# Strassen output product on one core: the loads of k, v and q queued behind the turns of q

## The chip, the core and the metric

The kernel runs on one core of one Trainium2 chip. The metric is device time in microseconds (us), the lower the better. A core has a matrix engine (TensorE, PE in the profile, with its weight loads as PEld), a vector engine (VectorE, DVE), an activation engine (ScalarE, ACT), a general engine (GpSimd, POOL) and an engine that here only issues transfers (SyncE, SP). Each works through its own instructions in order and waits on semaphores for the others. Transfers (DMAs), plain ones and those that transpose, are issued from the queues of these engines and are carried out by 16 DMA engines.

## The reference

```python
# q, k, v: (8, 8, 576, 64) float32; w_in: (512, 2048); w_out: (2048, 512)
k_p = k.reshape(B, H, 72, 8, D).mean(axis=3)
v_p = v.reshape(B, H, 72, 8, D).mean(axis=3)
scores = scale * np.matmul(q, k_p.transpose(0, 1, 3, 2))
scores = scores - np.max(scores, axis=-1, keepdims=True)
attn = np.exp(scores)
attn = attn / (np.sum(attn, axis=-1, keepdims=True) + 1e-09)
x = np.matmul(attn, v_p)          # then (B*S, H*D) = (4608, 512)
h = x @ w_in
out = (h - np.tanh(h)) @ w_out    # (4608, 512) float32
```

## The kernel before

The work has two parts that run beside each other: attention, batch by batch (8 batches of 576 rows, 8 heads), and a two-layer product, group by group (9 groups of 512 tokens). The attention output, turned so that features lie on partitions, is the tile xT, a ring of three groups. The first group and the first two batches are handled ahead of the loop; the rest is the loop `for g in range(1, NG)` (L926). A pass of this loop is called pass g below. In pass g the matrix engine computes group g, and the attention of batch nb = g + 1 is computed between its products; the raw inputs of batch nn = g + 2 are loaded. So passes 1 to 5 load, passes 1 to 6 do attention, and passes 7 and 8 only do their groups.

A pass on PE begins with the up projection: seven `h_pair` and two `h_one`, 64 matmuls (L529) of w1b by xT into PSUM. ACT takes the tanh (L541), DVE subtracts it and leaves Gt (L542). Then comes the output product, in 14 steps of u, eight matmuls each (L585): seven products of sums of blocks (Strassen's scheme) in place of eight. In steps 0 to 4, after the eight matmuls, `scores(nb, u)` runs: two halves of 288 columns of a score tile (L348), whose right-hand side is qT, then the exponentials on ACT (L367). In steps 6, 7, 8, 9 and 11 `av` computes 128 rows of the attention output each, and a DMA transpose from SP's queue (L433) turns it into xT. In step 6 POOL sums k and v of batch nn over the pools of 8 (`pool_k`, L247 to L255, then `pool_v`, L266 to L290). Stores of the group's output (L602) follow at the end of the pass.

A group has 512 tokens and a batch 576, so the up projection of pass g + 1 reads 448 - 64 g rows of batch g + 1 at the most: of the five turns of x that pass g issues, the first three are needed in pass 1 to 2, two in passes 3 and 4, one after that.

The order of all instructions is that of the program text (`manual_schedule`), engine by engine. What concerns the change is the queue of SP. In pass g it issues, in this order:

- at p = 0, `k_dma_transpose(nb)` (L331): one DMA that turns the summed k, kd, into kT, which POOL then places into KB for the scores (L299 to L303)
- at p = 0, if there is a batch nn, `load_k(nn)` (L137 of 1024 KB, L146 of 128 KB) and `load_v(nn)` (L137 of 1024 KB, L141 four times of 32 KB)
- at p = 2 (in pass 1 at p = 3, c being p - 1 there), `q_dma_transpose(nb)` (L203): five DMA transposes of q_bf into qT, one for each block of 128 or 64 rows of q
- there too, if there is a batch nn, `load_q(nn)` (L170 of 1024 KB, L162 of 128 KB)
- in the product steps the five turns of x (L433), then the stores (L602)

q_bf is the bf16 copy of q that ACT casts in three parts (`q_cast_part`, L192 and L197) ahead of `h_pair` for p = 0, 1, 2. The buffer of raw q, q_raw, is a single one; k_raw, v_raw, KB and qT have two buffers each.

Of the kernel before, what the change touches and what calls it, by code (L numbers as in the profile page):

```python
# [42 lines left out]
def kernel(  # L43
# [106 lines left out]
    def load_k(b):  # L150
        return [
            load_main(k_pairs, k_raw[b % 2], b, 0, NM),
            load_dense(k_pairs, k_raw[b % 2], b),
        ]

    def load_v(b):
        return [load_main(v_pairs, v_raw[b % 2], b, 0, NM)] + load_left(
            v_pairs, v_raw[b % 2], b
        )
# [6 lines left out]
    def load_q(b, tail=True):  # L166
        if b not in q_raws:
            q_raws[b] = raw.tile([128, H, R + 1, D], FP32, name="q_raw", tag="q_raw")
        t = q_raws[b]
        nc.sync.dma_start(  # L170
            out=t[:, :, 0:R, :], in_=q[b, :, 0:QA, :].rearrange("h (p j) d -> p h j d", j=R)
        )
        if tail:
            load_q_tail(b, t, nc.sync)
# [14 lines left out]
    def q_cast_part(b, n):  # L189
        t = q_raws[b]  # L190
        if n < 2:
            nc.scalar.copy(  # L192
                out=q_bf[:, 0:R, 4 * n : 4 * n + 4, :].rearrange("p j h d -> p h j d"),
                in_=t[:, 4 * n : 4 * n + 4, 0:R, :],
            )
        else:
            nc.scalar.copy(out=q_bf[:QT, R, :, :], in_=q_raws.pop(b)[:QT, :, R, :])  # L197

    def q_dma_transpose(b):
        qT = work.tile([128, NHP, S], BF16, name="qT", tag="qT")  # L200
        for j in range(R + 1):
            rows = 128 if j < R else QT
            nc.sync.dma_start_transpose(  # L203
                out=qT[:, :, j * 128 : j * 128 + rows],
                in_=q_bf[:rows, j, :, :].rearrange("p h d -> p (h d)"),
            )
        qTs[b] = qT
# [89 lines left out]
    def kb_main(kb, ps, t0, t1, engs):  # L297
        kv = kb.rearrange("p (t x) -> p t x", x=KP)
        engs[0](out=kv[0:D, t0:t1, 0:G], in_=ps[0:D, :, 0:G])  # L299
        engs[1](out=kv[D:128, t0:t1, G:128], in_=ps[D:128, :, G:128])  # L300

    def kb_left(kb, ps, eng):
        eng(  # L303
            out=kb[D:128, :].rearrange("p (t x) -> p t x", x=KP)[:, :, 128 : 128 + LO],
            in_=ps[D:128, 0 : NM * LO].rearrange("p (x t) -> p t x", t=NM),
        )
# [22 lines left out]
    def k_dma_transpose(b):  # L329
        kT = work.tile([128, NT, 128], BF16, name="kT", tag="kT", bufs=1)  # L330
        nc.sync.dma_start_transpose(  # L331
            out=kT[:, :, :], in_=kdups.pop(b)[:, :, :, :].rearrange("p t a d -> p (t a d)")
        )
        kTs[b] = kT

    def k_place(b, eng):
        kT = kTs.pop(b)
        kb_main(KB[b % 2], kT[:, 0:NM, :], 0, NM, (eng, eng))
        kb_left(KB[b % 2], kT[:, NM, :], eng)
# [197 lines left out]
    def h_pair(g, p, b0, ts):  # L537
        h_mms(g, p, PS[:, b0, :])
        h_mms(g, p + NP, PS[:, b0 + 1, :])
        t2 = TS[:, 2 * ts : 2 * ts + 2, :]  # L540
        nc.scalar.activation(out=t2, in_=PS[:, b0 : b0 + 2, :], func=ACT.Tanh)  # L541
        nc.vector.tensor_sub(out=Gt[:, p, :, :], in0=PS[:, b0 : b0 + 2, :], in1=t2)  # L542

    def h_one(g, p, s, b0, ts):
        h_mms(g, p + s * NP, PS[:, b0, :])
        nc.scalar.activation(out=TS[:, ts, :], in_=PS[:, b0, :], func=ACT.Tanh)
        nc.vector.tensor_sub(out=Gt[:, p, s, :], in0=PS[:, b0, :], in1=TS[:, ts, :])  # L547

    def sum_p(a, b):
        nc.vector.tensor_tensor(  # L550
            out=P[:, a:b, :], in0=Gt[:, a:b, 0, :], in1=Gt[:, a:b, 1, :], op=ALU.add
        )

    def sum_q(a, b):
        nc.vector.tensor_tensor(
            out=Q[:, a:b, :], in0=Gt[:, a:b, 0, 0:HT], in1=Gt[:, a:b, 1, HT:TG], op=ALU.add
        )
# [9 lines left out]
    def w_sum(out, a, b, op, eng=nc.vector, k0=0, k1=NP):  # L567
        return eng.tensor_tensor(
            out=out[:, k0:k1, :], in0=a[:, k0:k1, :], in1=b[:, k0:k1, :], op=op
        )  # L570
# [10 lines left out]
    def product(g, bk, lhs, rhs, k0, k1, first, tts=(0, 1)):  # L581
        apart = g == NG - 1 and bk == C1
        for k in range(k0, k1):
            for tt in tts:
                nc.tensor.matmul(  # L585
                    part(g, bk, tt),
                    lhsT=lhs(k, slice(tt * 128, (tt + 1) * 128)),
                    rhs=rhs[:, k, :],
                    start=(first and k == 0 and (tt == 0 or apart)),
                    stop=(k == NP - 1),  # L590
                    skip_group_check=True,
                )
# [6 lines left out]
    def store(g, th, tts=(0, 1), c0=0, c1=DM):  # L599
        for tt in tts:  # L600
            for n, (r0, r1, dst) in enumerate(out_segments(g * TG + th * HT + tt * 128, 128)):
                nc.sync.dma_start(out=dst[:, c0:c1], in_=O[r0:r1, 2 * th + tt, c0:c1])  # L602
# [14 lines left out]
    def after_product(g, n):  # L617
        if n == 0:
            nc.scalar.copy(out=m4, in_=chain(g, C1))
        if n == 1:  # L620
            nc.vector.tensor_tensor(out=O[:, 2:4, 0:HD], in0=chain(g, C2), in1=m4, op=ALU.add)  # L621
            sum_d(0, 2)
            sum_d(2, 4)
        if n == 2:
            nc.scalar.copy(out=m45, in_=chain(g, C1))
            nc.gpsimd.tensor_tensor(out=m4, in0=O[:, 2:4, 0:HD], in1=m45, op=ALU.subtract)  # L626
            sum_d(4, 6)
            sum_d(6, 8)
        if n == 3:
            nc.vector.tensor_tensor(out=O[:, 0:2, HD:DM], in0=m4, in1=chain(g, C2), op=ALU.subtract)  # L630
        if n == 4:
            nc.scalar.copy(out=m451, in_=chain(g, C1))  # L632
            nc.vector.tensor_tensor(out=m451, in0=m451, in1=m45, op=ALU.subtract)
        if n == 5:
            nc.vector.tensor_tensor(
                out=O[:, 2:4, HD:DM], in0=m451, in1=chain(g, C2), op=ALU.subtract
            )
# [288 lines left out]
    for g in range(1, NG):  # L926
        nb = g + 1 if g + 1 < B else None
        nn = g + 2 if g + 2 < B else None
        for p in range(NP - 1):
            c = p if g > 1 else p - 1  # L930
            if nb is not None and 0 <= c < 3:
                q_cast_part(nb, c)
            h_pair(g, p, (0, 2, 4, 6, 0, 2, 4)[p], p % 2)
            if g == 1 and p < 4:
                w_sum(w2s[:, 0, :, :], b11, b22, ALU.add, k0=2 * p, k1=2 * p + 2)
            if p >= 4:
                sum_p(2 * p - 8, 2 * p - 6)
            if nb is not None and p == 0:
                k_dma_transpose(nb)
                k_place(nb, nc.gpsimd.tensor_copy)  # L940
                if nn is not None:
                    load_k(nn)
                    load_v(nn)
            if nb is not None and c == 2:
                q_dma_transpose(nb)
                if nn is not None:
                    load_q(nn)
        h_one(g, NP - 1, 1, 0, 2)
        h_one(g, NP - 1, 0, 1, 3)
        sum_p(6, 8)  # L950
        sum_q(0, 4)
        sum_q(4, 8)
        ps_a = Banks(2, 3, 4, 5, 0, 1)
        for u in range(14):
            n, half = u // 2, u % 2
            bk, lhs, rhs = products[n]
            if n == 6 and g == NG - 1:
                break
            product(g, bk, lhs, rhs, 4 * half, 4 * half + 4, n < 2)
            if half:  # L960
                after_product(g, n)
                if g == 1 and n in (1, 2):
                    w_sum(w2s[:, 2, :, :], b21, b22, ALU.add, k0=4 * n - 4, k1=4 * n)
            if nb is not None:
                if u < NT:
                    scores(nb, u)
                if u in (6, 7, 8, 9, 11):
                    av(nb, (6, 7, 8, 9, 11).index(u), ps_b1, True)
                if u == 6 and nn is not None:
                    pool_k(nn, nc.gpsimd)  # L970
                    pool_v(nn, nc.gpsimd)
            if u == 12:
                store(g, 1)
        if g < NG - 1:
            nc.scalar.copy(out=O[:, 0:2, 0:HD], in_=chain(g, C1))
            store(g, 0)
# [43 lines left out]
```

## Time and profile before

| | us |
|---|---|
| runs shown, median of 3 (lowest to highest) | 334.75 (333.26 to 337.02) |
| profiled execution, its own time | 335.3 |
| profiled execution, span from first to last instruction | 333.6 |
| PE busy in the span | 291.2 (87%) |
| DVE busy | 228.9 (69%) |
| ACT busy | 154.3 (46%) |
| POOL busy | 122.4 (37%) |

The mean granted clock of PE over the span was 0.946 of full speed. Times in the trace count from the first instruction. The profile gives for each instruction its start, its duration, its engine and its line; an idle time in square brackets names what ended it. `SPq` rows are DMAs as SP issues them: their duration is that of the issue, not of the transfer. A clock of 1.00 in the rows is 2.4 GHz and 0.50 is 1.2 GHz.

### The profile page before, as it was taken

What the parts mean: (1) busy time and instruction counts of PE and PEld (TensorE: products, weight loads), DVE (VectorE), ACT (ScalarE), POOL (GpSimd) and SP (SyncE); (2) the same over time, 40 slices, a digit from 0 to 9 for tenths busy, and PEclk for the clock granted to TensorE, in tenths of its full rate; (3) what the DMA queues carried; (4) which work ended last, traced back from release to release, by engine and by line L of the source; (5) the groups of instructions that cost most, each with busy time, mean ns of one, the idle gap of its engine ahead of it and who ended that gap; (6) DMA issues with size and microseconds to landing.
All of it is one profiled execution on the core that took longest, in us unless ns stands there. A gap on an engine that the chain in (4) does not pass through costs nothing.

```text
span 333.6 us, 5456 instructions
## 1 busy us (share of the span) xinstructions
PE 291.2 (87%) x2040; PEld 183.4 (55%) x2040; DVE 228.9 (69%) x400; ACT 154.3 (46%) x244; POOL 122.4 (37%) x122
## 2 busy tenths in 40 slices
PE   7999999999893799929996499939998999999990
PEld 2454455458541586417843286417944874684680
DVE  6458668899777087853969077763969767945970
ACT  3656774863462335614174235625085425325410
POOL 8404459804940059300971049400981100020010
PEclk9999999999998599987999599987999999999996
DMA  7999999991379614894279823894255044003004
GB/s 264 205 244 262 290 285 298 284 207 26 73 179 294 168 27 118 266 182 124 49 169 284 187 42 74 250 233 143 47 145 99 2 84 116 0 33 95 0 2 126
DMA packets 66378, 49.84 MB, mean 149 GB/s; under 512 B 39984, under 2 KB 53296, under 8 KB 66352
## 3 DMA queue, kind: packets, MB, share of 16 engines
q1 hardware_dynamic: 59024, 42.94, 49.2%
q0 software_dynamic: 4752, 4.72, 8.5%
q10 hardware_dynamic: 2576, 1.84, 2.0%
q8 instruction: 16, 0.26, 0.3%
q14 instruction: 10, 0.08, 0.1%
HBM read 36.70 MB, written 9.44 MB: 138 GB/s over the span
## 4 chain that ended last, share of the span: by engine, by line
PE 43%; DMA 16%; DVE 14%; POOL 11%; SPq 6%; issue 4%; ACT 3%; ACTq 1%; POOLq 0%
PE PS L585 19%; DMA v_raw<-in_v_dram 11%; PE PS L529 10%; DVE Gt L542 5%; PE PS L511 4%; DMA qT<-q_bf 3%; PE PS L348 3%; POOL v_raw L266 3%; POOL k_raw L247 3%; DVE Dg L560 2%; PE PS L395 2%; PE PS L483 2%; DMA q_raw<-in_q_dram 2%; SPq L602 2%; DVE P L550 2%
## 5 line engine op out<-in xcount | busy, mean ns | idle before, releaser
L529 PE MATMUL PS<-xT,w1b 128*128 128x512 bf16 x512 | 111.8, 379 | 1.5 <-DMA xT<-x_sb 0.9
L542 DVE TENSOR_TENSOR Gt<-PS,TS 128x1024 bf16<-128x1024 f32 x56 | 68.4, 1221 | 29.7 <-ACT TS L541 29.7
L529 PEld LDWEIGHTS <-w1b 128*128 128x128 f16 x512 | 49.9, 98 | 60.6 <-DMA xT<-x_sb 1.1
L541 ACT ACTIVATE TS<-PS 128x1024 f32<-128x1024 f32 x56 | 57.4, 1025 | 31.5 <-PE PS L529 28.2
L626 POOL TENSOR_TENSOR m<-O,m 128x512 f32<-128x512 f32 x8 | 11.1, 1388 | 154.9 <-DVE Dg L560 89.8
L348 PE MATMUL PS<-qT,KB 128*128 128x288 bf16 (+5 forms) x128 | 20.9, 316 | 28.3 <-DMA qT<-q_bf 28.0
L367 ACT ACTIVATE E<-PS 128x288 bf16<-128x288 f32 x60 | 22.0, 410 | 41.1 <-PE PS L348 41.0
L413 DVE TENSOR_TENSOR x_sb<-PS,rden 128x256 bf16<-128x256 f32 x72 | 30.5, 424 | 2.5
L621 DVE TENSOR_TENSOR O<-PS,m 128x512 f32<-128x512 f32 x8 | 5.5, 690 | 38.4 <-ACT E L367 38.1
L585 PEld LDWEIGHTS <-Gt 128*128 128x128 bf16 x256 | 26.1, 104 | 9.1 <-DVE Gt L547 2.1
L585 PE MATMUL PS<-w2s,Dg 128*128 128x256 f16 x256 | 30.2, 272 | 0.0
L585 PEld LDWEIGHTS <-P 128*128 128x128 bf16 x256 | 26.4, 105 | 6.7 <-issue 1.4
L247 POOL TENSOR_TENSOR k_raw<-k_raw 128x512 f32<-128x512 f32 (+2 forms) x13 | 21.6, 1681 | 16.1 <-DMA k_raw<-in_k_dram 16.1
L348 PEld LDWEIGHTS <-KB 128*128 128x128 bf16 (+1 forms) x128 | 7.8, 102 | 34.4 <-issue 25.6
L585 PEld LDWEIGHTS <-Dg 128*128 128x128 bf16 x256 | 24.6, 98 | 2.8 <-issue 0.2
L550 DVE TENSOR_TENSOR P<-Gt 128x1024 bf16<-128x1024 bf16 x32 | 21.9, 683 | 0.3
L585 PE MATMUL PS<-w2s,Gt 128*128 128x256 f16 x128 | 20.3, 310 | 1.3 <-DVE Gt L547 1.3
L560 DVE TENSOR_TENSOR Dg<-Gt 128x1024 bf16<-128x1024 bf16 x32 | 21.0, 717 | 0.0
L395 PE MATMUL PS<-VB,E 128*128 128x130 bf16 x240 | 20.2, 220 | 0.1
L585 PE MATMUL PS<-w2b,P 128*128 128x256 f16 x128 | 19.5, 306 | 0.0
L266 POOL TENSOR_TENSOR v_raw<-v_raw 128x512 f32<-128x512 f32 (+1 forms) x12 | 19.2, 1620 | 0.0
L632 ACT COPY m<-PS 128x512 f32<-128x512 f32 x8 | 4.7, 586 | 29.5 <-PE PS L585 29.5
(108 smaller groups left out, 396.4 us busy)
## 6 DMA issues: line engine op xcount, KB each, us to landing
k_raw<-in_k_dram SPq DMA_DIRECT2D x7, 1024.0 KB, 6.2
q_raw<-in_q_dram SPq DMA_DIRECT2D x7, 1024.0 KB, 5.9
v_raw<-in_v_dram SPq DMA_DIRECT2D x7, 1024.0 KB, 8.6
out_dram<-O SPq DMA_DIRECT2D x36, 128.0 KB, 2.4
out_dram<-O SPq DMA_DIRECT2D x16, 256.0 KB, 2.8
w1b<-in_moe_w_in_dram POOLq DMA_DIRECT2D x4, 512.0 KB, 13.7
w2b<-in_moe_w_out_dram POOLq DMA_DIRECT2D x4, 512.0 KB, 17.5
k_raw<-in_k_dram SPq DMA_DIRECT2D x7, 128.0 KB, 6.0
```

Source lines behind the costliest of these rows:

```text
L247: first = eng.tensor_tensor(out=r[:, ta:tb, 0:4, :], in0=r[:, ta:tb, 0:4, :], in1=r[:, ta:tb, 4:8, :], op=ALU.add)
L266: eng.tensor_tensor(out=r[:, ta:tb, 0:4, :], in0=r[:, ta:tb, 0:4, :], in1=r[:, ta:tb, 4:8, :], op=ALU.add)
L348: nc.tensor.matmul(dst[p : p + w], lhsT=KB[b % 2][:, o : o + w], rhs=qTs[b][:, m, c0:c1], start=True, stop=True,)
L367: nc.scalar.activation(out=E[:, t, half * hs : (half + 1) * hs], in_=ps[:, :], func=ACT.Exp, scale=SCALE)
L395: nc.tensor.matmul(ps[:, 2 * n : 2 * n + 2, :].rearrange("p h d -> p (h d)") if n < 2 else ps.rearrange("p (a s) d -> p a s d", s=2)[:, :, ...
L413: nc.vector.tensor_tensor(out=x_sb[:, half, :, :], in0=ps[:, :, 0:D], in1=rden[:, :, :].to_broadcast([128, 4, D]), op=ALU.mult,)
L529: nc.tensor.matmul(dst, lhsT=w1b[:, fb, i * 128 : (i + 1) * 128], rhs=xT[:, fb, c0 : c0 + TG], start=(fb == 0), stop=(fb == NFB - 1),)
L541: nc.scalar.activation(out=t2, in_=PS[:, b0 : b0 + 2, :], func=ACT.Tanh)
L542: nc.vector.tensor_sub(out=Gt[:, p, :, :], in0=PS[:, b0 : b0 + 2, :], in1=t2)
L550: nc.vector.tensor_tensor(out=P[:, a:b, :], in0=Gt[:, a:b, 0, :], in1=Gt[:, a:b, 1, :], op=ALU.add)
L560: nc.vector.tensor_tensor(out=Dg[:, a:b, :, :], in0=Gt[:, a:b, :, 0:HT], in1=Gt[:, a:b, :, HT:TG], op=ALU.subtract,)
L585: nc.tensor.matmul(part(g, bk, tt), lhsT=lhs(k, slice(tt * 128, (tt + 1) * 128)), rhs=rhs[:, k, :], start=(first and k == 0 and (tt == 0 o ...
```

## The change

The calls that load k and v of batch nn move from p = 0, behind the turn of k, to the place where q is turned, behind its five transposes and ahead of the load of q. Nothing else differs.

```diff
             if nb is not None and p == 0:
                 k_dma_transpose(nb)
                 k_place(nb, nc.gpsimd.tensor_copy)
+            if nb is not None and c == 2:
+                q_dma_transpose(nb)
                 if nn is not None:
                     load_k(nn)
                     load_v(nn)
-            if nb is not None and c == 2:
-                q_dma_transpose(nb)
-                if nn is not None:
                     load_q(nn)
```

## Rows read from the trace of the kernel before

**Rows 1.** Waits of PE: who waited for whom, us in total, times, longest.

```profile
PE PS L348 <- DMA qT<-q_bf: 28.0, 9, 6.8
...
PE PS L529 <- DMA xT<-x_sb: 0.9, 1, 0.9
```

**Rows 2.** Passes 1 to 6 as windows: start:end, us, busy by engine, PEclk, DMA share, GB/s.

```profile
56.52:87.89 31.37, 29.77 (x223) 19.52 (x223) 29.86 (x46) 16.46 (x27) 17.49 (x15) 1.00 0.66 164
87.89:128.05 40.16, 32.32 (x223) 21.04 (x224) 24.64 (x44) 15.63 (x25) 16.01 (x15) 0.87 0.60 149
128.05:165.95 37.90, 31.94 (x224) 20.84 (x222) 24.80 (x44) 16.45 (x26) 15.66 (x16) 0.91 0.63 158
165.95:204.39 38.44, 31.10 (x224) 20.44 (x222) 24.79 (x44) 16.45 (x26) 15.66 (x16) 0.91 0.62 155
204.39:241.52 37.13, 31.50 (x224) 20.59 (x222) 24.80 (x44) 16.45 (x26) 15.66 (x16) 0.91 0.60 160
241.52:272.16 30.64, 29.39 (x224) 19.71 (x222) 24.73 (x48) 16.43 (x26) 9.74 (x11) 1.00 0.37 82
```

**Rows 3.** Timeline of PE, pass 3: start, us, line, operation, count, idle before.

```profile
147.81 0.40 PE L348 MATMUL PS<-qT,KB 128*128 128x288 bf16 x1 [4.91 <-DMA qT<-q_bf]
149.26 0.40 PE L348 MATMUL PS<-qT,KB 128*128 128x288 bf16 x1 [1.05 <-DMA qT<-q_bf]
```

**Rows 4.** Two stretches of pass 3 as windows, columns as in rows 2.

```profile
138.00:144.00 6.00, 4.90 (x27) 2.42 (x25) 6.00 (x8) 3.13 (x4) 0.00 (x0) 1.00 1.06 357
...
149.00:150.00 1.00, 0.74 (x4) 0.51 (x4) 0.00 (x0) 0.31 (x1) 0.00 (x0) 0.50 0.45 132
```

**Rows 5.** Timeline of SP: turns of k in passes 2 to 6, pass 3's loads.

```profile
96.26 1.27 SPq L331 DMA_TRANSPOSE kT<-kd  x1
...
133.76 1.27 SPq L331 DMA_TRANSPOSE kT<-kd  x1
135.07 0.58 SPq L137 DMA_DIRECT2D k_raw<-in_k_dram  x1
...
139.30 8.81 SPq L203 DMA_TRANSPOSE qT<-q_bf  x5
...
173.02 1.27 SPq L331 DMA_TRANSPOSE kT<-kd  x1
...
210.75 1.25 SPq L331 DMA_TRANSPOSE kT<-kd  x1
...
248.78 1.25 SPq L331 DMA_TRANSPOSE kT<-kd  x1
```

**Rows 6.** The chain that ended last, passes 3 and 6: start, us, what.

```profile
136.38 9.24 DMA v_raw<-in_v_dram
145.64 1.19 SPq L203
146.92 2.29 DMA qT<-q_bf
...
255.37 2.33 DMA qT<-q_bf
```

**Rows 7.** Waits of SP's queue, columns as in rows 1.

```profile
SPq L203 <- DMA v_raw<-in_v_dram: 6.4, 5, 1.6
```

**Rows 8.** DMAs issued between 131 and 152 us: count, size, median us to landing.

```profile
k_raw<-in_k_dram SPq DMA_DIRECT2D x1, 1024.0 KB, 6.5
...
qT<-q_bf SPq DMA_TRANSPOSE x5, 4.8
```

**Rows 9.** Timeline of PE, pass 6, columns as in rows 3.

```profile
257.74 0.30 PE L348 MATMUL PS<-qT,KB 128*128 128x288 bf16 x1 [1.25 <-DMA qT<-q_bf]
```

**Rows 10.** Timeline around the end of pass 3: who uses what was loaded.

```profile
159.38 3.04 POOL L247 TENSOR_TENSOR k_raw<-k_raw 128x512 f32<-128x512 f32 x2
159.76 8.80 SPq L433 DMA_TRANSPOSE xT<-x_sb  x5
...
166.63 1.05 ACT L192 CAST q_bf<-q_raw 128x1024 bf16<-128x1024 f32 x1
```

## The prediction

> **What bounds the kernel now.** I read the waits of TensorE (PE) first, since a new order in a queue can only pay where the engine that carries the chain stands still. There is one large wait: the score matmuls (L348) wait for qT, the turned q, 28.0 us in 9 waits, nearly a tenth of the run. The only other one that matters here is a single 0.9 us for xT [rows 1].
>
> Next, where it falls. I cut the run at the first up-projection matmul of each pass of the loop over g; call that moment H, and H' the same moment of the following pass. Passes 2 to 5 take 40.16, 37.90, 38.44 and 37.13 us at a mean granted clock of 0.87 to 0.91. Pass 6, which turns q as they do but loads nothing, takes 30.64 us at clock 1.00, and pass 1 takes 31.37 [rows 2]. So some 31 us of the run set four passes apart from pass 6. In pass 3 the wait is seen directly: after the first eight product matmuls PE stands 4.91 us before the first half of the first score tile and 1.05 us before the second [rows 3]. Then it runs on at a granted clock of 0.50, that is 1.2 of 2.4 GHz [rows 4].
>
> Then, why qT is late: the DMA queue on SyncE (SP). In pass 3 the turn of k is issued at 133.76; the loads of k and v follow from 135.07; the first turn of q starts only at 139.30 [rows 5]. The turns then stall again. The load of v goes out at 136.38 and takes 9.24 us; at 145.62 it has landed, and at 145.64 the fourth turn of q begins; the fifth starts at 146.92 and lands 2.29 us later, and PE goes on [rows 6]. The waits of SP name it: turns of q waiting for v's load, 5 times, for the five passes that load [rows 7]. Counted along SP's DMAs, the fourth turn is the eighth after that load, and the second turn is the eighth after the main load of k (landed at 135.07 + 6.5 = 141.57 [rows 5, 8]): each DMA seems to wait for the one eight places ahead of it. The transposes that are issued also crawl: median 4.8 us to landing in pass 3 [rows 8], where the last one of pass 6, with no load around it, needs 2.33 [rows 6].
>
> **What the change does, step by step.** In passes 1 to 5 SP's order becomes: turn of k, five turns of q, then k (2 DMAs), v (5), q (2). No instruction is added or removed; seven loads per pass move behind five transposes, q's two stay last, all still on SP; POOL's, ACT's and PE's streams stay as they are.
>
> *The turns of q.* With no load ahead the sequence is that of pass 6: turn of k at 248.78, fifth turn of q at 255.37, landed 2.33 later at 257.70, that is 8.92 us from the turn of k [rows 5, 6]. Eight places ahead of each turn now lie stores and turns of x of the pass before, as in pass 6.
>
> *When PE wants them.* In pass 6 PE asked for the second half at 257.74 - 1.25 = 256.49, that is H + 14.97, and waited 1.25 [rows 9, 2]. Without that wait a pass takes 30.64 - 1.25 = 29.39. The turns of k stand at H + 8.37, 5.71, 7.07 and 6.36 in passes 2 to 5 (96.26 - 87.89 and so on; the number of stores ahead of them differs) [rows 5, 2]. These offsets hang on the end of the pass before, whose order is untouched, so I keep them. Adding 8.92, qT lands at H + 17.29, 14.63, 15.99 and 15.28; PE waits 2.32, 0, 1.02 and 0.31.
>
> *The sum.* Pass 2: 29.39 + 2.32 = 31.71, saving 8.45. Pass 3: 29.39, saving 8.51. Pass 4: 30.41, saving 8.03. Pass 5: 29.70, saving 7.43. Together 32.4. About a quarter of it is clock: of pass 3's 8.51, 5.96 is the two waits [rows 3] and 2.55 the matmuls that ran slowly after them. The 2.32 us left in pass 2 lie between a wait of 1.25 that kept the clock (pass 6: 1.00) and one of 5.96 that halved it; if it halves, pass 2 loses up to 2.55 again. I take no loss, as the nearer row is pass 6, and keep 2.55 for the range. Pass 1 has nothing to give back: PE's nine waits for qT are two in each of passes 2 to 5 and one in pass 6. Passes 6 to 8 are unchanged. The profiled execution took 335.3 us with a span of 333.6; 335.3 - 32.4 = 302.9. It lies 0.55 above the median of the runs, so I forecast 302.5.
>
> *What is late next: the loads.* Their first, k, now goes out one spacing of transposes (146.92 - 145.64 = 1.28 [rows 6]) after the fifth turn: 6.59 + 1.28 = 7.87 after the turn of k, at H + 16.2, 13.6, 14.9 and 14.2, instead of 1.31 after it. From k's issue to v's landing it took 10.55 us (135.07 to 145.62 [rows 5, 6]); q's 1.18 MB add 3.3 at the 357 GB/s of the busy stretch [rows 4]: 13.85 in all. At most it is 17.05, if q adds as much as k took to land, 6.5 [rows 8]. Who needs them: POOL's sum over k starts 6.57 before H' (159.38 against 165.95), ACT's first cast of q 0.68 after H' [rows 10, 2]. With H' at H + 31.71, 29.39, 30.41 and 29.70, k lands (issue + 6.5) 2.4 to 2.7 us before it is wanted, and q 2.3 to 2.7 before, or 0.5 to 0.9 late by the upper bound, at most 3.5 over four passes. So I take 0: hidden, with little to spare. One wait is added: q's small second load now stands eight behind k's main load, and SP holds there until k has landed. Queued behind it on SP are the turns of x, first issued at H' - 6.19 [rows 10], which is later than that (k lands over 2.4 us before H' - 6.57); cost 0.
>
> *A rule against this.* The Trainium skill (DMA: Bandwidth & Descriptors, Rules for kernel authors) says to issue a DMA early and to wait on it late, which would keep the loads in front. The trace shows the early issue paid for by PE's 28 us [rows 1]. By the rule the loads' lost cover would come off the gain, and the step above finds 0 to 3.5 us of that.
>
> **Rivals.** *A: the turns of x take over the wait.* They are now issued while the tail of v and q still moves. Transposes behind loads took 4.8 instead of 2.33 [rows 8, 6], 2.5 more each, and PE has once waited 0.9 for xT [rows 1]. For it: the loads end only some 2 us before H'. Against: PE needs only the first two or three of the five turns at H'. Price: 2 us in each of four passes, 311; with the clock halved each time (2.55 more) up to 321. The Trainium skill (same page, Queues, rings and completion order) has each DMA engine take descriptors in ring order; the turns of q agree (4.8), and for turns of x behind loads no run here shows it.
>
> *B: the loads are not the cause.* If turns of q are slow by themselves, nothing changes: about 335. Against it: pass 6, and the pairs around 141.57 and 145.62 above.
>
> *C: slower.* ACT's first cast of q stands ahead of the first tanh of the next pass. If the loads, sharing the DMA engines with turns and stores, come so late that this cast waits, the gain of a pass (8.1 in the mean) is used up once they are 2.3 + 8.1 = 10.4 us later than I put them. That takes loads of 24 us instead of 13.85; at 27 the run would be 335.3 + 4 x 2.8 = 346. No row shows loads at that pace.
>
> **How the numbers follow.** Forecast 0.72, A 0.19, B 0.05, C 0.04. Faster by over 1% (about what a measurement can tell from no change) is the forecast and A: 0.91; within 1% is B: 0.05; slower is C: 0.04. The range: downwards, the remaining waits (3.65 us) could go in part: 300. Upwards, pass 2's clock, the late q and the cheaper half of A: 311.
>
> **What would show it.** Right: turns of q begin 1.3 us after the turn of k in passes 2 to 5; SP's waits at L203 for v are gone; these passes take 29 to 32 us at clock 1.00; PE's wait for qT falls to about 5 us. A is right if PE waits for xT at the start of passes, C if ACT waits for q at L192, B if transposes still take 4.8 us with no load ahead. A time above 311 or below 300 makes the prediction wrong.

## The result and the profile after

The changed kernel takes 305.82 us (median of 4 runs, 303.93 to 307.88); the kernel before, on the same chip, 334.0 (4 runs, 332.24 to 337.02). The ratio is 0.9149, 95% interval 0.9057 to 0.9241. The profiled execution took 307.88 us with a span of 306.2; its counterpart of before took 335.3 with 333.6.

The page of the kernel after: the busy time of each engine, and the granted clock in 40 slices.

```profile
PE 282.6 (92%) x2040; PEld 179.3 (59%) x2040; DVE 230.3 (75%) x400; ACT 154.1 (50%) x244; POOL 121.3 (40%) x122
...
PEclk9999999999999899999999999999999999999997
```

PE does the same 2040 matmuls in 282.6 us instead of 291.2, at a mean clock of 0.989 instead of 0.946. The rest of the gain is waiting. Waits of the kernel after (who waited for whom, us in total, times, longest), against [rows 1]:

```profile
PE PS L348 <- DMA qT<-q_bf: 5.7, 5, 2.6
PE PS L529 <- DMA xT<-x_sb: 3.8, 2, 3.0
```

PE's wait for qT fell from 28.0 to 5.7. The wait for xT rose from 0.9 to 3.8: a second one, of 2.95, has come. Passes 1 to 6 of the kernel after as windows, with the columns of [rows 2]:

```profile
55.53:86.96 31.43, 29.77 (x222) 19.56 (x223) 29.98 (x46) 16.33 (x27) 17.54 (x15) 1.00 0.70 179
86.96:121.27 34.31, 31.05 (x223) 20.55 (x223) 24.63 (x44) 15.63 (x25) 15.50 (x15) 0.95 0.73 174
121.27:151.51 30.24, 29.56 (x224) 19.63 (x222) 25.18 (x45) 16.61 (x27) 16.04 (x16) 1.00 0.83 198
151.51:184.72 33.21, 29.55 (x223) 19.64 (x223) 25.76 (x47) 17.76 (x28) 18.31 (x17) 1.00 0.92 181
184.72:214.20 29.48, 29.39 (x223) 19.66 (x224) 23.45 (x39) 14.78 (x24) 12.60 (x13) 1.00 0.81 201
214.20:244.91 30.71, 29.39 (x225) 19.70 (x223) 24.73 (x48) 16.42 (x26) 9.78 (x11) 1.00 0.37 82
```

Passes 2 to 5 take 127.24 us together, where they took 153.63: 26.4 of the 27.4 us by which the two profiled executions differ. Pass 5 stands at the floor of 29.39 that the prediction worked out from pass 6. Passes 2 and 4 do not, and the timeline of PE after shows why (start, us, line, operation, count, idle before):

```profile
102.50 0.28 PE L348 MATMUL PS<-qT,KB 128*128 128x288 bf16 x1 [0.67 <-DMA qT<-q_bf]
105.36 0.40 PE L348 MATMUL PS<-qT,KB 128*128 128x288 bf16 x1 [2.58 <-DMA qT<-q_bf]
...
136.70 0.30 PE L348 MATMUL PS<-qT,KB 128*128 128x288 bf16 x1 [0.46 <-DMA qT<-q_bf]
...
167.19 0.30 PE L348 MATMUL PS<-qT,KB 128*128 128x288 bf16 x1 [0.70 <-DMA qT<-q_bf]
```

Pass 2 still waits 3.25 us for qT, and its 0.40 us matmul at 105.36 runs at half the clock, as the one in [rows 3] did. Pass 4 waits 0.70 for qT; its other loss is the 2.95 us for xT ahead of H at 184.72. SP's timeline after, passes 2 to 4, against [rows 5]:

```profile
95.91 1.26 SPq L331 DMA_TRANSPOSE kT<-kd  x1
97.30 6.92 SPq L203 DMA_TRANSPOSE qT<-q_bf  x5
104.28 0.57 SPq L137 DMA_DIRECT2D k_raw<-in_k_dram  x1
...
126.97 1.26 SPq L331 DMA_TRANSPOSE kT<-kd  x1
128.34 7.22 SPq L203 DMA_TRANSPOSE qT<-q_bf  x5
135.60 0.58 SPq L137 DMA_DIRECT2D k_raw<-in_k_dram  x1
...
158.21 1.27 SPq L331 DMA_TRANSPOSE kT<-kd  x1
159.59 6.41 SPq L203 DMA_TRANSPOSE qT<-q_bf  x5
166.04 0.58 SPq L137 DMA_DIRECT2D k_raw<-in_k_dram  x1
```

The turns of q begin 1.4 us after the turn of k in place of 5.5, and SP gets through them in 6.4 to 7.2 us in place of 8.8. The chain that ended last after (start, us, what) has two steps that count:

```profile
134.37 2.29 DMA qT<-q_bf
...
177.79 6.79 DMA xT<-x_sb
```

The fifth turn of pass 3 lands at 136.66, 9.69 after the turn of k (before: 146.92 + 2.29 - 133.76 = 15.45). And the second turn of x of pass 4, one of the two that the next pass needs, took 6.79 us to land, the first 8.8: that is the new wait of pass 4.

### The profile page after: what moved, and what is told of

Its sections match the earlier page's. It is cut to its first block, busy times and chain, and to the rows that moved or that the text cites. A ratio compares the mean times of both kernels' runs of the same rounds, so it can differ in the third digit from the quotient of the medians.

```text
span 306.2 us, 5451 instructions
## 1 busy us (share of the span) xinstructions
PE 282.6 (92%) x2040; PEld 179.3 (59%) x2040; DVE 230.3 (75%) x400; ACT 154.1 (50%) x244; POOL 121.3 (40%) x122
## 4 chain that ended last, share of the span: by engine, by line
PE 60%; DMA 15%; DVE 12%; POOL 4%; ACT 3%; issue 3%; SPq 2%; ACTq 0%; POOLq 0%; DVEq 0%
PE PS L585 25%; PE PS L529 23%; DVE Gt L542 6%; DMA w1b<-in_moe_w_in_dram 4%; DMA qT<-q_bf 4%; PE PS L511 4%; DMA k_raw<-in_k_dram 4%; PE PS L348 3%; PE PS L395 3%; DMA xT<-x_sb 3%; DVE P L550 2%; ACT TS L541 2%; DVE w2s L568 1%; POOL k_raw L247 1%; SPq L203 1%
## 5 line engine op out<-in xcount | busy, mean ns | idle before, releaser
L529 PE MATMUL PS<-xT,w1b 128*128 128x512 bf16 x512 | 111.8, 379 | 4.7 <-DMA xT<-x_sb 3.8
L529 PEld LDWEIGHTS <-w1b 128*128 128x128 f16 x512 | 49.8, 98 | 64.2 <-issue 3.7
L585 PEld LDWEIGHTS <-Gt 128*128 128x128 bf16 x256 | 24.8, 99 | 8.8 <-DVE Gt L547 2.7
L247 POOL TENSOR_TENSOR k_raw<-k_raw 128x512 f32<-128x512 f32 (+2 forms) x13 | 21.6, 1679 | 16.8 <-DMA k_raw<-in_k_dram 16.8
L585 PEld LDWEIGHTS <-P 128*128 128x128 bf16 x256 | 24.8, 99 | 5.0 <-issue 1.4
L348 PE MATMUL PS<-qT,KB 128*128 128x288 bf16 (+5 forms) x128 | 18.1, 293 | 5.9 <-DMA qT<-q_bf 5.7
L560 DVE TENSOR_TENSOR Dg<-Gt 128x1024 bf16<-128x1024 bf16 x32 | 22.1, 750 | 0.0
L585 PE MATMUL PS<-w2s,Gt 128*128 128x256 f16 x128 | 18.0, 282 | 1.6 <-DVE Gt L547 1.5
L395 PEld LDWEIGHTS <-E 128*128 128x128 bf16 x240 | 16.8, 98 | 1.9 <-issue 0.4
L585 PE MATMUL PS<-w2b,P 128*128 128x256 f16 x128 | 16.6, 276 | 0.0
L974 ACT COPY O<-PS 128x512 f32<-128x512 f32 x7 | 4.1, 586 | 24.6 <-PE PS L585 24.6
## 6 DMA issues: line engine op xcount, KB each, us to landing
q_raw<-in_q_dram SPq DMA_DIRECT2D x7, 1024.0 KB, 10.2
```

Of the source, the lines that this page charges most:

```text
L247: first = eng.tensor_tensor(out=r[:, ta:tb, 0:4, :], in0=r[:, ta:tb, 0:4, :], in1=r[:, ta:tb, 4:8, :], op=ALU.add)
L348: nc.tensor.matmul(dst[p : p + w], lhsT=KB[b % 2][:, o : o + w], rhs=qTs[b][:, m, c0:c1], start=True, stop=True,)
L395: nc.tensor.matmul(ps[:, 2 * n : 2 * n + 2, :].rearrange("p h d -> p (h d)") if n < 2 else ps.rearrange("p (a s) d -> p a s d", s=2)[:, :, ...
L529: nc.tensor.matmul(dst, lhsT=w1b[:, fb, i * 128 : (i + 1) * 128], rhs=xT[:, fb, c0 : c0 + TG], start=(fb == 0), stop=(fb == NFB - 1),)
L560: nc.vector.tensor_tensor(out=Dg[:, a:b, :, :], in0=Gt[:, a:b, :, 0:HT], in1=Gt[:, a:b, :, HT:TG], op=ALU.subtract,)
L585: nc.tensor.matmul(part(g, bk, tt), lhsT=lhs(k, slice(tt * 128, (tt + 1) * 128)), rhs=rhs[:, k, :], start=(first and k == 0 and (tt == 0 o ...
```

## The experiments

### Is it the wait eight places ahead? (e1)

In the kernel before, the small loads of v go first, so that behind each turn's eighth place ahead there is no longer a main load of k or v.

```diff
                 if nn is not None:
+                    load_left(v_pairs, v_raw[nn % 2], nn)
                     load_k(nn)
-                    load_v(nn)
+                    load_main(v_pairs, v_raw[nn % 2], nn, 0, NM)
```

> The kernel before, with the four small loads of v issued first, then k, then v's main load, all still ahead of the turns of q. The same DMAs; only now what stands eight places ahead of each turn is the turn of k or a small load. Theory 'the wait on the DMA eight ahead is what holds the turns': they issue without a stop 5.4 to 11.8 us after the turn of k, the fifth lands 12.9 after it instead of 15.4, so passes 2 to 5 lose 2.5 us of wait each and some slow clock: about 320. Theory 'the turns stand behind the loads' data, whenever they are issued': loads end some 13 to 14 us after the turn of k, the fifth turn lands 14 to 15.5 after it: 328 to 335, not told from before.

It took 334.04 us, ratio to before 1.0004 (0.9966 to 1.0042), as the second theory had it. The waits of SP at L203 for v, [rows 7], are gone, and nothing came of it. SP's and PE's rows in pass 3 of this kernel:

```profile
132.38 1.27 SPq L331 DMA_TRANSPOSE kT<-kd  x1
...
138.65 8.23 SPq L203 DMA_TRANSPOSE qT<-q_bf  x5
```
```profile
147.32 0.40 PE L348 MATMUL PS<-qT,KB 128*128 128x288 bf16 x1 [5.80 <-DMA qT<-q_bf]
```

The five turns still take 8.23 us to issue (6.4 to 7.2 after the change) and PE still stands 5.80 us, 28.1 in all. So the wait that the prediction read in [rows 6, 7] was there, but costs nothing by itself: without it the turns are as slow. The reason has to be what the loads do to the turns, or the room that they take ahead of them on SP.

### Traffic, or SP's time? (e3 and e9)

Two kernels take one of the two away. The first is the kernel after, with the main loads of k and v issued by POOL (in the program's text ahead of the turn of k), so that SP goes straight on to the turns while the bytes move.

```diff
             if nb is not None and p == 0:
+                if nn is not None:
+                    for src, dst in ((k_pairs, k_raw), (v_pairs, v_raw)):
+                        nc.gpsimd.dma_start(out=dst[nn % 2][:, 0:NM, :], in_=src[nn, 0:128, 0:NM, :])
                 k_dma_transpose(nb)
...
                 if nn is not None:
-                    load_k(nn)
-                    load_v(nn)
+                    load_dense(k_pairs, k_raw[nn % 2], nn)
+                    load_left(v_pairs, v_raw[nn % 2], nn)
```

> The kernel after, but the main loads of k and v (1024 KB each) go out from POOL's queue ahead of the turn of k; the small ones stay behind the turns on SP. So the bulk of k and v moves while the turns of q are issued, as in before, but from another queue. Theory 'it is the place in SP's queue': turns begin 1.3 us after the turn of k and land within 3 us each, passes 2 to 5 stay within 1.5 us of those of after: 304 to 309. Theory 'it is the traffic, wherever it is issued': turns take about 4.8 us to landing, qT lands about 2.5 us later than in after in passes 2 to 5, with the clock lost again in some: 315 to 325.

The second is the kernel before, with SP issuing the seven loads where it did, but the two main ones bringing an eighth of their bytes; the rest of k and v is left out.

```diff
                 if nn is not None:
-                    load_k(nn)
-                    load_v(nn)
+                    n = POOL * D // 8
+                    nc.sync.dma_start(
+                        out=k_raw[nn % 2][:, 0:NM, 0:n], in_=k_pairs[nn, 0:128, 0:NM, 0:n]
+                    )
+                    load_dense(k_pairs, k_raw[nn % 2], nn)
+                    nc.sync.dma_start(
+                        out=v_raw[nn % 2][:, 0:NM, 0:n], in_=v_pairs[nn, 0:128, 0:NM, 0:n]
+                    )
+                    load_left(v_pairs, v_raw[nn % 2], nn)
```

> The kernel before, with the order of before, but the main loads of k and v bring only an eighth of their bytes (the rest of k and v is left out, so the output is another one). The same DMAs in the same order, hardly any traffic. Theory 'traffic beside the turns makes them late, whatever the queue': the turns run at their free pace, the fifth lands some 13 us after the turn of k instead of 15.4 (4.2 us of SP's own issuing of seven loads stay ahead of it), passes 2 to 5 lose 2.5 us of wait and some slow clock: 318 to 326. Rival 'SP's issuing alone makes them late': within 2% of before, over 328. Rival 'bytes alone': close to after, under 310.

POOL's queue: 334.75 us, ratio 1.0015 (0.9974 to 1.0056): no gain, and slower than either theory had said (304 to 309, 315 to 325). Small bytes: 326.89 us, ratio 0.9771 (0.9737 to 0.9805): 2.3% faster than before, and between the 318 to 326 of 'traffic' and the 328 of 'issuing'. SP's and POOL's timelines in pass 3 with POOL's queue, and that kernel's DMAs issued between 136 and 152 us (count, median us to landing):

```profile
136.41 1.28 SPq L331 DMA_TRANSPOSE kT<-kd  x1
137.80 8.88 SPq L203 DMA_TRANSPOSE qT<-q_bf  x5
```
```profile
137.94 0.80 POOL L941 DMA_DIRECT2D k_raw<-in_k_dram  x1
138.73 0.75 POOL L941 DMA_DIRECT2D v_raw<-in_v_dram  x1
```
```profile
qT<-q_bf SPq DMA_TRANSPOSE x5, 7.5
```

SP's timeline in pass 3 with small bytes, and that kernel's DMAs between 130 and 150 us:

```profile
132.10 1.27 SPq L331 DMA_TRANSPOSE kT<-kd  x1
133.41 0.58 SPq L943 DMA_DIRECT2D k_raw<-in_k_dram  x1
...
138.73 6.44 SPq L203 DMA_TRANSPOSE qT<-q_bf  x5
```
```profile
qT<-q_bf SPq DMA_TRANSPOSE x5, 2.5
```

With POOL's queue the turns start as early as after the change, even ahead of the bulk, and crawl: 8.88 us to issue, a median of 7.5 to landing (4.8 in [rows 8]). No load stands ahead of them in their own queue. With small bytes they run at a free pace, 6.44 and 2.5, but start 5.32 us later (133.41 to 138.73), for that long SP spends on issuing seven loads (3.9 to 5.3 in passes 2 to 5). From the turn of k to the landing of the last turn of q, in pass 3 of each kernel (for before also in pass 6, which has no loads), worked out as above; 145.45 + 4.86 - 136.41 with POOL's queue and 143.98 + 2.29 - 132.10 with small bytes:

| kernel | us | loads ahead on SP | main loads moving |
|---|---|---|---|
| before, pass 6 | 8.92 | no | no |
| after | 9.69 | no | no |
| POOL's queue | 13.90 | no | yes |
| small bytes | 14.17 | yes | an eighth of them |
| before | 15.45 | yes | yes |

So in pass 3 either cause alone makes 5.0 to 5.3 us, and both together 6.5: they overlap, and taking away one gives little. Pass 3 is where the two kernels show most. Over passes 2 to 5, counted to the score matmul that waits for the last turn and against pass 6, POOL's queue makes 3.4 to 5.0 us, small bytes 3.9 to 5.3, and both together (before) 5.6 to 6.6.

In passes 2 to 5 both kernels saved about the same, 7.7 us with POOL's queue (153.63 - 145.89) and 7.3 with small bytes (153.63 - 146.29). With POOL's queue pass 1 lost it again: POOL issues there at 64.09, beside the last turns of q, one of them took 8.70 us to land, and pass 1 grew from 31.37 to 37.80. In this kernel the turn of k crawls as well: in pass 2 it took 8.8 us to land, POOL placed it into KB late, and PE stood 4.04 us for KB.

What follows: the prediction's picture of turns held up in one queue was half of it. Turns crawl beside bulk from POOL's queue as they do beside bulk from their own. The Trainium skill (DMA: Bandwidth & Descriptors, Issuing engines are not separate DMA queues) says that transfers run on the same 16 DMA engines and interleave whichever engine started them; these rows agree. By its sentence on ring order alone, which the prediction weighed, the turns would have been free when the bulk went to another queue; 7.5 against 4.8 us says that this order isn't all that sets their pace. POOL's descriptors are of another kind (software), so how much of the 7.5 belongs to that is not told apart.

### How little there is to spare for the loads (e5)

The kernel after, with the loads of k, v and q later still: k's waits for the sum that DVE makes behind the second product, v and q follow.

```diff
     def after_product(g, n):
         if n == 1:
-            nc.vector.tensor_tensor(out=O[:, 2:4, 0:HD], in0=chain(g, C2), in1=m4, op=ALU.add)
+            o_done[g] = nc.vector.tensor_tensor(
+                out=O[:, 2:4, 0:HD], in0=chain(g, C2), in1=m4, op=ALU.add
+            )
...
                 after_product(g, n)
+                if n == 1 and nn is not None:
+                    after(load_k(nn), o_done[g])
+                    load_v(nn)
+                    load_q(nn)
```

> The kernel after, but the loads of k, v and q wait until DVE has added the second product (about 18.5 us into a pass), that is 2.5 to 5 us later than in after. It asks how much room the moved loads have. Theory of the prediction: 2.3 to 2.7 us of room, so k, q and the turns of x come late by 0 to 3 us in each of passes 1 to 5, partly hidden: 309 to 322, with PE waiting for xT at the start of passes and ACT for q. Rival 'there is far more room than that': within 1% of after, 303 to 309.

It took 334.25 us, ratio to before 1.0005 (0.997 to 1.004): the whole gain is gone, more than either theory had said (309 to 322, 303 to 309). The loads went out at H + 20.7 to 21.7, that is 3.4 to 9.0 us later than after the change (H + 17.3, 14.3, 14.5, 12.7), more than had been meant. Its waits:

```profile
PE PS L529 <- DMA xT<-x_sb: 22.0, 4, 6.2
...
ACT q_bf L192 <- DMA q_raw<-in_q_dram: 15.3, 5, 3.5
...
PE PS L529 <- DMA q_raw<-in_q_dram: 4.6, 1, 4.6
```

No wait for qT is left, and PE stands as long for xT instead: 5.16 to 6.24 us at the ends of passes 1 to 4, after which the clock halves as it did before (passes 2 to 5: 0.91 to 0.92). The fifth wait, 4.6 us at the end of pass 5, the view puts down to a load of q. But L529 reads xT and no q, and the turn of x that went out at 230.61 took 8.0 us to land, which is 238.6, when PE went on (238.68): this wait too is for xT. It is rival A in full, reached once the loads run into the turns of x. Of rival C it shows that ACT waits for q, 15.3 us in all, beside A's waits; what that alone would cost is not told apart.

### The same kernel once more (e0)

> The kernel after once more, for a second trace of it: in the first, PE waited 2.95 us for xT at the end of pass 4 and passes took 34.3, 30.2, 33.2 and 29.5 us. If that wait is a fixed cost of the new order it stands there again; if it hangs on small shifts between loads and turns of x, it is elsewhere or gone, and the time lies between 303 and 308.

307.13 us in one execution, beside 334.6 for before. Passes 2 to 4 as windows:

```profile
87.77:121.98 34.21, 31.38 (x223) 20.56 (x224) 24.79 (x44) 15.61 (x25) 16.03 (x15) 0.95 0.72 175
121.98:153.30 31.32, 29.55 (x222) 19.61 (x223) 25.98 (x48) 17.68 (x28) 16.95 (x16) 1.00 0.84 194
153.30:183.73 30.43, 29.55 (x222) 19.63 (x223) 24.36 (x42) 15.81 (x27) 15.13 (x14) 1.00 0.94 193
```

Pass 2 repeats itself, 34.21 at clock 0.95. Pass 4's wait of 2.95 for xT does not. The pass takes 30.43, which meets the forecast of 30.41 by luck: the wait for qT that the forecast had in it is not there. Instead PE stands 1.29 us at the end of pass 3 and 0.79 at the end of pass 4, and the view puts both down to DVE's x_sb.

The turns of x are slow here too, though. In pass 3 the second one, which the next pass needs, went out at 147.35 and took 5.8 us; it landed at 153.15, and x_sb was done at 153.25, just before PE started at 153.30. So PE would have waited there even without DVE. Pass 2 stands in both traces; slow turns of x do too, and how much PE loses by them differs.

### Taking the rest away (e6, e8, and both)

What still keeps qT late after the change is the stores of the pass before: they stand ahead of the turn of k on SP (in pass 2 eight of them, from 89.46, for 6.34 us). Two edits, alone and together. The first issues the stores of group g - 1 behind the turns of q of pass g, ahead of the loads.

```diff
                 q_dma_transpose(nb)
+                if g > 1:
+                    store(g - 1, 1)
+                    store(g - 1, 0)
...
-            if u == 12:
+            if u == 12 and g + 2 >= B:
                 store(g, 1)
...
-            store(g, 0)
+            if g + 2 >= B:
+                store(g, 0)
```

> The kernel after, but the stores of groups 1 to 5 are issued behind the turns of q of the following pass instead of ahead of its turn of k; k, v and q follow them. Theory: what is left of PE's wait for qT comes from the stores ahead of the turn of k in SP's queue; without them the fifth turn lands some 11.6 us into the pass, before PE asks at 14.97, the clock stays, and passes 2 to 6 take 29.4 to 29.7 each: 296 to 300. Rival: the loads now end later against a shorter pass, the turns of x run into them and PE waits for xT instead: 303 to 309.

312.58 us, ratio to before 0.9351 (0.9282 to 0.9419): slower than after, and above what theory and rival had said (296 to 300, 303 to 309). PE's wait for qT is gone, and one for xT has its place:

```profile
PE PS L529 <- DMA xT<-x_sb: 10.0, 4, 4.3
```

With qT on time PE also asks for the next group earlier, while the loads, now behind the stores too, come no sooner. What tells these kernels apart is the room from the issue of k's load to the moment at which PE wants the next xT, which is the pass less its wait for xT and less the offset of the load. In passes 2 to 5 it is 12.9, 16.0, 15.9 and 15.5 us here, and the waits for xT are 4.30, 2.35, 2.52 and none. After the change it is 17.0, 15.9, 15.7 and 16.8, with 2.95 in the third alone; in e5 10.4 in passes 2 to 4, with 5.16 to 6.24. So at 13 us and less PE waits each time, at 16.8 and more it doesn't, and at 15.5 to 16.0 it waits in three cases of five. It is no sharp limit, but the change sits on that edge.

The second edit brings k's load a pass sooner, between the fourth and fifth turn of x, into the buffer that is then free.

```diff
                 if nn is not None:
-                    load_k(nn)
+                    if g == 1:
+                        load_k(nn)
                     load_v(nn)
...
+                if u == 10 and g + 3 < B:
+                    load_k(g + 3)
```

> The kernel after, but from pass 1 on the load of k for the pass after next is issued between the fourth and the fifth turn of x, where no transpose is urgent; behind the turns of q only v and q are left, 2.4 of 3.5 MB. Theory 'the room for loads between the turns of q and the turns of x is what is short': the turns of x run free, PE's wait for xT at the ends of passes 2 to 5 falls to 0, the wait for qT stays: 302 to 305. Rival 'k's load now meets the stores and the turn of k': qT comes later by 1 to 3 us in passes 2 to 5, clock halved in more than one: 308 to 320.

312.18 us, ratio to before 0.9313 (0.9267 to 0.9359), again slower than after, as the rival had it (308 to 320). Now xT is free (one wait of 0.9, as before), but the load of k meets the stores and the turn of k. DMAs issued between 118 and 147 us:

```profile
out_dram<-O SPq DMA_DIRECT2D x3, 256.0 KB, 4.9
...
kT<-kd SPq DMA_TRANSPOSE x1, 5.6
```

Stores take 4.9 in place of 2.6 and the turn of k 5.6 in place of 2.9 (medians of before between 131 and 152 us); PE waits 10.2 us for qT, and the granted clock of passes 2 and 5 falls to 0.90 and 0.95. Both edits together:

> The stores behind the turns of q as in the earlier experiment, and k's load early as in its neighbour. Theory 'room': no wait for qT, and with 1.2 MB less behind the turns the loads end 3.4 us earlier than with the stores alone, so that PE's 10 us of wait for xT fall to 0 to 3: 298 to 302. Rival: k's load beside the turns of k and q costs what it saves: 305 to 313.

299.4 us (298.99 to 300.9), ratio to before 0.8955 (0.8916 to 0.8993): faster than both kernels, and what the theory had said. Passes 2 to 5:

```profile
87.36:117.65 30.29, 29.57 (x223) 19.64 (x224) 25.39 (x47) 16.10 (x27) 16.28 (x15) 1.00 0.90 198
117.65:147.91 30.26, 29.55 (x223) 19.62 (x223) 24.78 (x44) 16.30 (x27) 15.64 (x15) 1.00 0.95 197
147.91:177.39 29.48, 29.39 (x223) 19.67 (x224) 24.06 (x42) 15.73 (x25) 14.87 (x15) 1.00 0.85 202
177.39:206.87 29.48, 29.39 (x225) 19.69 (x223) 24.80 (x44) 16.32 (x26) 15.65 (x16) 1.00 0.83 202
```

No wait for qT is left, xT costs 2.1 in three waits, and passes 4 and 5 stand 0.09 above the floor. Each edit alone moves the wait to the other transposes. That the two together work is not because turns and bulk no longer meet. In pass 3 k's load goes out at 117.84 and moves beside the turns of k and q (DMAs issued between 117 and 135 us):

```profile
k_raw<-in_k_dram SPq DMA_DIRECT2D x1, 1024.0 KB, 5.9
...
kT<-kd SPq DMA_TRANSPOSE x1, 4.5
```

The turn of k takes 4.5 us to land, against 2.9 before. But without stores ahead of it, it goes out at H + 2.8 to 4.3 in place of H + 4.9 to 9.0, so even slowed turns of q are there before PE asks; and with k's load gone from behind them, q's main load lands 27.3 us into pass 3, where with the stores alone it landed 31.2 us into it. The turns of x that follow are still slow (the first 6.4 us), but PE loses only 0.64 by them there.

## Why the prediction was right, and where it was off

*The cause held.* The loads ahead of the turns of q were what held PE up: passes 2 to 5 became 26.4 us shorter, the turns start 1.4 us behind the turn of k, the waits at L203 for k and v are gone, and what is left of the wait for qT (5.7) is what "about 5" had said. The time of 305.82 lies 3.3 above the forecast of 302.5, inside the range. One sign that the prediction named did not hold in full: passes 2 and 4 took 34.31 and 33.21 us and not 29 to 32, the first of them at clock 0.95 and not 1.00.

*"Each DMA seems to wait for the one eight places ahead"*: seen, but not the cause; e1 removed it at no gain. The two causes that count are SP's issuing (5.3 us alone in pass 3, 3.9 to 5.3 over passes 2 to 5) and traffic (5.0, and 3.4 to 5.0). The forecast didn't depend on which, since the change takes both away.

*The sum* came out 5.0 short (307.88 against 302.9 for the profiled execution). Two passes make it:

- Pass 2: 34.31 against 31.71. The offset that was to be kept, H + 8.37, became 8.95, and the 8.92 from turn of k to landing became 9.41 (the fifth turn went out at 103.04 and landed 2.28 later; 105.32 - 95.91): the wait is 3.25, not 2.32. Then the clock: the two lines of PE's busy time, 31.05 against 29.39, make 1.66. The prediction had this term ("up to 2.55"), took no loss by pass 6 as the nearer row, and kept it for the range; both profiles of the kernel after say that it should have stood in the sum.
- Pass 4: 33.21 against 30.41, nearly all of it the 2.95 for xT. "Hidden, with little to spare" was right for POOL and ACT, which waited for no load of k or q on the way, and the loads took about what the sum gave them: 13.4 to 15.4 us from k's issue to the last landing of q, where it had 13.85 and at most 17.05. What the sum left out is the turns of x, which rival A had at 2 us a pass in all four. The wait of 2.95 came once in one trace; in the other PE stood 1.29 and 0.79 us at two such places.
- Pass 3, 30.24 against 29.39: the 8.92 became 9.69, so the turn came 0.46 late. Pass 5, 29.48 against 29.70, and 0.99 less ahead of pass 1 than before make up a little.

*The added wait*, SP's hold for k ahead of q's small load, is there after the change (8.5 us in 6 waits at L162), and cost nothing, as worked out: the turns of x came later anyway (3.7 us behind that load in pass 3, 141.19 to 144.93).

*The rule to issue early* (the Trainium skill, DMA: Bandwidth & Descriptors, Rules for kernel authors): the runs show both sides. The kernel before paid for its early loads with 26.4 us over four passes, because transposes that were wanted at once stood behind and beside them; e5 shows that a load 3.4 to 9 us later than here costs as much.

*The rivals.* B fell. A is real and close. The prediction had no row for turns of x behind loads; after the change, in all four passes, the first turn of x took 4.3 to 8.8 us and landed 1.0 to 3.3 us after q's main load, which was issued ahead of it. PE lost by that only in pass 4; e5 and e6 show the wait whole and in part. C didn't come with the change, and when e5 brought the loads that late, A's wait came first.

## What to carry to other kernels

Transposing DMAs that an engine waits for want either a stretch with little bulk or the time to be slow in: count both what stands ahead of them on the issuing engine and what bulk moves beside them, from whichever queue. A load that is moved out of the way of one set of turns is moved towards the next one, so look up, before moving it, how many microseconds lie between its landing and that next set. And where two edits each only move a wait, try them together before giving up either: alone these two took 312.58 and 312.18 us, together 299.4.

## What the runs showed of the hardware

The two causes don't add: in pass 3 5.3 and 5.0 us alone, 6.5 together. With the bulk on another queue transposes beside it were slower, not faster (in pass 3 a median of 7.5 us against 4.8).

The clock doesn't follow the length of one wait. After the change PE waited 2.95 us for xT ahead of pass 5, and the granted clock stayed 1.00; in pass 2 it waited 0.67 and 2.58 with 0.28 us of matmul between, and the clock fell. Short windows of the kernel after, around these two, columns as in [rows 2]:

```profile
102.00:105.00 3.00, 0.28 (x1) 0.19 (x2) 2.97 (x6) 0.41 (x1) 0.00 (x0) 1.00 0.35 68
...
106.00:107.00 1.00, 1.00 (x6) 0.74 (x5) 0.00 (x0) 0.20 (x1) 0.00 (x0) 0.50 0.91 268
...
109.00:110.00 1.00, 1.00 (x12) 0.87 (x10) 0.00 (x0) 0.70 (x2) 0.00 (x0) 1.00 0.90 270
```
```profile
184.70:186.00 1.30, 1.28 (x6) 0.60 (x7) 0.00 (x0) 0.00 (x0) 1.30 (x1) 1.00 0.53 99
```

In pass 2 the engine ran at 0.50, 1.2 GHz, for some 3 us behind the waits and then at 2.4 GHz again. The kernel with the stores behind the turns (e6) has two single waits for xT that differ by 0.17 us. After the shorter one the granted clock fell (0.79 and 0.56 in the next 5 us) and the up projection took 15.66 us; after the longer one it stayed at 1.00:

```profile
155.11 15.66 PE L529 MATMUL PS<-xT,w1b 128*128 128x512 bf16 x62 [2.35 <-DMA xT<-x_sb]
...
188.96 13.97 PE L529 MATMUL PS<-xT,w1b 128*128 128x512 bf16 x62 [2.52 <-DMA xT<-x_sb]
```

So which of the two it will be was not to be read from the length of the wait.

Two things stay open. Why the first two turns of x took 8.8 and 6.8 us in pass 4 of one trace of the kernel after, where the first ones of the other loading passes took 4.2 to 7.0 in the two traces, wasn't found. And how the DMA engines share themselves between transposes and bulk can't be seen in these traces; only the landing times can.
